# A new head for an attention and two-layer kernel: finer first chunks from two queues, norms and softmax beside the scores, two blocks interleaved

## The chip, the core and the metric

The kernel runs on one core of one Trainium2 chip. Its time is the device time of one execution in microseconds (us); the number given for a kernel is the median of several executions. A profiled execution stands beside it: the hardware profiler records every instruction of the engines (TensorE, called PE in the rows, its weight loads PEld; VectorE, DVE; ScalarE, ACT; GpSimd, POOL; and the queue of SyncE, SPq) and every packet of the DMA engines.

## The reference

Everything is in float32. Attention is over the channels, not the tokens: with N = 6016 tokens and C = 256 channels, the scores are a 256x256 matrix, summed over all tokens. Two gated layers follow, token by token.

```python
def _attn_ref(q, k, v, tau):            # q, k, v: 1 x 6016 x 256
    qn = q / (np.linalg.norm(q, axis=1, keepdims=True) + 1e-06)
    kn = k / (np.linalg.norm(k, axis=1, keepdims=True) + 1e-06)
    s = kn.transpose(0, 2, 1) @ qn / tau
    s = s - s.max(-1, keepdims=True)
    a = np.exp(s)
    a /= a.sum(-1, keepdims=True) + 1e-09
    return (v @ a).astype(np.float32)

def _moe_ref(x, w_gate, w_val, w_out, rms_g):    # 256 -> 1536 -> 256
    rms = np.sqrt(np.mean(x * x, axis=-1, keepdims=True) + 1e-06)
    xn = x / rms * rms_g
    g = xn @ w_gate
    silu = g * (1.0 / (1.0 + np.exp(-g)))
    val = xn @ w_val
    return (silu * val @ w_out).astype(np.float32)

def _moe2_ref(x, w_in, w_out):                   # 256 -> 2048 -> 256
    h = x @ w_in
    g = h - np.tanh(h)
    return (g @ w_out).astype(np.float32)
```

## The kernel before

**Scores (L276 to L349).** q and k lie with 47 tokens on each of the 128 partitions. A tile is one token per partition, 128 x 256 of q and of k. A chunk is 1, 2 or 4 tiles, loaded by one DMA for q and one for k, all from SP's queue, with four buffers each. For each tile TensorE multiplies k's two halves of 128 channels with q (L308); each float32 product runs as two passes on the engine, so a tile is four passes. Beside it ACT squares the chunk (L325) and DVE adds the squares into `acc` (L326), which has room for 4 tiles; at the end `acc` is folded to 2 tiles (L328), and products with a column of ones (L345) give the squared norms of the channels in `nrm`. The products for the last two chunks stand behind the norm products. DVE turns the norms into reciprocals with an integer seed and three Newton steps (`rsqrt_ops`, L93 to L96) on 128x8 numbers.

**Softmax (L363 to L392).** The reciprocal norms of q have to lie along the free dimension. DVE scales an identity by them (`dq`), a product with ones spreads them to all partitions (L370), ACT copies them to SBUF. Then for the two halves of the rows in turn: scale, row maximum, exponential with row sum, reciprocal of the sum, scale. The result is `a_full`.

**The weights.** They come as 64-bit floats seen as pairs of 32-bit integers, in chunks of 512 columns. The generator `conversion` (L172) makes float32 of them and splits each into a high and a low half, in steps: ACT `w_start` (L136), DVE shift (L183), DVE `w_low` of the chunk before (L78), DVE and/or (L189), DVE shift/or (L195), ACT high half (L75). `pump(n)` issues n steps; the table `PLAN` says how many stand at which label (`at("s", i)` after score chunk i, `at("c", k)` in the middle part, `at("g", ...)`, `at("h", ...)` in the layers). `need(...)` issues steps until the weights it names exist: the gate asks for the column block two ahead. The order of the chunks is wg0, wv0, w10, wg1, wv1, w11, wg2, ... `W_LOADS` says after which score chunks the first five are loaded.

**The middle part (L654 to L692) and the layers.** The tokens are cut into 12 blocks of 512. For blocks 0 and 1 x = v a is a full float32 product (L412); ACT squares it, narrow products (L479) give the mean squares per token, DVE the reciprocal root, and again an identity scaled on DVE (`diag`, L491) and a product with ones (L497) spread it. The normalised x is split into a high and a low half (`x0h`, `x0l`; block 1 `x1h`, `x1l`), and each product of the layers is three products of halves (`mm3`, L82 to L84). The gate runs column by column, block 0 three columns ahead of block 1; the steps of block 1's x (`post`) are issued between the columns of block 0, so many after each as `POST` says. Every engine executes its instructions in the order in which they are written. At most 8 DMAs are under way at once; the one that takes a completion counter waits for the one that had it.

What the prediction speaks of is in these functions:

Of the kernel before, what the change touches and what calls it, by code (L numbers as in the profile page):

```python
# [16 lines left out]
P = 128  # L17
# [15 lines left out]
def attn_moe_kernel(  # L33
# [132 lines left out]
    LAST_CHUNKS, FOLD = [4, 2, 1], 1  # L166
    BEHIND = 2
    W_LOADS = [1, 3, 5, 9, 11]
# [107 lines left out]
    def attention():  # L276
        with ExitStack() as st:
# [3 lines left out]
            for n in [1, 2, 1] + [W] * ((NT - W - 1) // W - 1) + LAST_CHUNKS:  # L281
                chunks.append((t, n))
                t += n
            assert t == NT
            H = W // 2
# [3 lines left out]
            S = [psum(f"S{m}") for m in range(KC)]  # L289
            raw = {}  # L290
            NCH = len(chunks)
# [11 lines left out]
            def scores(i):  # L303
                n = chunks[i][1]
                qt, kt = raw.pop(i)
                for j in range(n):
                    for m in range(KC):
                        nc.tensor.matmul(  # L308
                            S[m][:, :C], kt[:, j, m * P:(m + 1) * P], qt[:, j, :],
                            start=(i == 0 and j == 0), stop=(i == NCH - 1 and j == n - 1))  # L310
# [6 lines left out]
            nrm = psum("nrm")  # L317
            for i, (t0, n) in enumerate(chunks):
                for s in range(2):
# [6 lines left out]
                    nc.vector.tensor_add(out=acc[:, s, :n], in0=acc[:, s, :n], in1=sq[:, :n])  # L326
                if t0 + n == NT - sum(LAST_CHUNKS[FOLD:]):
# [467 lines left out]
```

## Time and profile before

| | |
|---|---|
| runs | 1206.48, 1207.55, 1207.74 us; median 1207.55 |
| profiled execution | 1206.14 us, its span 1204.30 us |
| PE busy | 1186.8 us (99% of the span) |
| DVE busy | 681.1 us (57%) |
| ACT busy | 536.2 us (45%) |
| DMA, first 10 us / 20 to 30 us | 215 / 416 GB/s |

The span is what the engines' records cover; 1.84 us of the execution lie around it. The busy shares are means over 1204 us; the change is in the first 100 us, where DVE is busy for 7 to 9 of every 10 us and the DMA engines are full from 12 to 40 us.

### The profile page before, as it was taken

How to read it: one execution, taken by the hardware profiler on the slowest of the kernel's cores; microseconds unless marked ns; L12 is line 12 of the kernel's file. 1: busy time of each engine (PE TensorE's matmuls, PEld its weight loads, DVE VectorE, ACT ScalarE, POOL GpSimd, SP SyncE). 2: the span in 40 equal slices, each digit the busy share in tenths (PEclk: the TensorE clock that was granted, in tenths of full speed). 3: DMA queues.
4: the chain of work that ended last, by engine and by line, in shares of the span. 5: the costliest groups of instructions: out<-in, count | busy, mean ns of one | idle time of the engine just before them, and what ended most of it. 6: DMA issues, size and time to landing. Idle time of an engine off the chain costs nothing.

```text
span 1204.3 us, 13571 instructions
## 1 busy us (share of the span) xinstructions
PE 1186.8 (99%) x5310; PEld 988.9 (82%) x5310; DVE 681.1 (57%) x1119; ACT 536.2 (45%) x930; POOL 0.7 (0%) x6
## 2 busy tenths in 40 slices
PE   8889999999999999999999999999999999999998
PEld 6668888888888888888888888888888888888998
DVE  5888779653384384375356347347337437436534
ACT  6556556543343354254344344344335325425434
POOL 0000000000000000000000000000000000000000
PEclk9999999999999999999999999999999999999999
DMA  9534332001001000000000000100100000000000
GB/s 340 208 107 123 89 104 88 18 19 35 1 1 36 1 1 20 16 1 18 18 1 18 18 1 1 35 1 1 35 1 1 32 1 1 18 1 1 18 1 14
DMA packets 20640, 43.33 MB, mean 36 GB/s; under 512 B 1889, under 2 KB 3169, under 8 KB 20577
## 3 DMA queue, kind: packets, MB, share of 16 engines
q1 hardware_dynamic: 20576, 42.48, 10.5%
q8 instruction: 41, 0.67, 0.2%
q14 instruction: 23, 0.18, 0.0%
HBM read 36.31 MB, written 6.16 MB: 35 GB/s over the span
## 4 chain that ended last, share of the span: by engine, by line
PE 97%; DVE 1%; DMA 1%; ACT 0%; issue 0%; SPq 0%; DVEq 0%
PE h L84 7%; PE h L82 7%; PE out L82 7%; PE out L84 7%; PE out L83 7%; PE h L83 7%; PE g L82 5%; PE y L84 5%; PE y L82 5%; PE g L84 5%; PE y L83 5%; PE g L83 5%; PE v L82 5%; PE v L84 5%; PE v L83 5%; PE S L308 3%
## 5 line engine op out<-in xcount | busy, mean ns | idle before, releaser
L546 DVE TENSOR_TENSOR t<-t,v 128x512 f32<-128x512 f32 (+1 forms) x144 | 97.4, 676 | 227.9 <-PE v L84 219.4
L560 DVE TENSOR_TENSOR t<-h,t 128x512 f32<-128x512 f32 (+1 forms) x192 | 129.6, 675 | 48.9 <-ACT t L559 48.8
L545 ACT ACTIVATE t<-g 128x512 f32<-128x512 f32 (+1 forms) x144 | 84.6, 588 | 129.5 <-PE g L84 126.5
L559 ACT ACTIVATE t<-h 128x512 f32<-128x512 f32 (+1 forms) x192 | 110.5, 575 | 17.3 <-PE h L84 17.1
L308 PE MATMUL S<-q,k 128*128 128x256 f32 x188 | 43.9, 394 | 5.5 <-DMA k<-k_in 5.5
L308 PEld LDWEIGHTS S<-q,k 128*128 128x128 f32 x188 | 36.7, 198 | 11.9 <-DMA q<-q_in 4.3
L326 DVE TENSOR_TENSOR acc<-acc,sq 128x1024 f32<-128x1024 f32 (+2 forms) x24 | 26.4, 1113 | 14.7 <-ACT sq L325 14.3
L96 DVE SCALAR_TENSOR_TENSOR y<-sq,y 128x512 f32<-128x512 f32 (+1 forms) x27 | 18.0, 668 | 0.0
L93 DVE SCALAR_TENSOR_TENSOR sq<-y,sq 128x512 f32<-128x512 f32 (+1 forms) x27 | 18.0, 668 | 0.0
L95 DVE TENSOR_TENSOR sq<-sq,y 128x512 f32<-128x512 f32 (+1 forms) x27 | 18.0, 667 | 0.0
L325 ACT ACTIVATE sq<-q 128x1024 f32<-128x1024 f32 (+2 forms) x12 | 11.6, 967 | 11.3 <-DMA q<-q_in 9.3
L443 ACT ACTIVATE xg<-x,g_t 128x512 f32<-128x512 f32 (+1 forms) x24 | 15.9, 667 | 1.1 <-PE ms L479 1.1
L75 ACT ACTIVATE u_2h<-t 128x512 fp32r<-128x512 f32 (+1 forms) x12 | 7.5, 623 | 18.5 <-DVE t L546 18.5
L75 ACT ACTIVATE w_12h<-t 128x512 fp32r<-128x512 f32 (+1 forms) x12 | 7.5, 623 | 18.5 <-DVE t L560 14.4
L75 ACT ACTIVATE u_8h<-t 128x512 fp32r<-128x512 f32 (+1 forms) x12 | 7.5, 623 | 18.2 <-DVE t L546 18.2
L75 ACT ACTIVATE u_1h<-t 128x512 fp32r<-128x512 f32 (+1 forms) x12 | 7.5, 623 | 18.1 <-DVE t L546 18.1
L75 ACT ACTIVATE u_6h<-t 128x512 fp32r<-128x512 f32 (+1 forms) x12 | 7.5, 623 | 18.1 <-DVE t L546 18.1
L75 ACT ACTIVATE u_9h<-t 128x512 fp32r<-128x512 f32 (+1 forms) x12 | 7.5, 624 | 17.7 <-DVE t L546 17.7
L75 ACT ACTIVATE u_7h<-t 128x512 fp32r<-128x512 f32 (+1 forms) x12 | 7.5, 623 | 17.7 <-DVE t L546 17.7
L75 ACT ACTIVATE u_10h<-t 128x512 fp32r<-128x512 f32 (+1 forms) x12 | 7.5, 623 | 17.7 <-DVE t L546 17.7
L75 ACT ACTIVATE u_0h<-t 128x512 fp32r<-128x512 f32 (+1 forms) x12 | 7.5, 623 | 17.3 <-DVE t L546 17.3
L75 ACT ACTIVATE u_5h<-t 128x512 fp32r<-128x512 f32 (+1 forms) x12 | 7.5, 624 | 17.2 <-DVE t L546 17.2
(2051 smaller groups left out, 3602.7 us busy)
## 6 DMA issues: line engine op xcount, KB each, us to landing
vraw<-vT_in SPq DMA_DIRECT2D x11, 512.0 KB, 3.8
outT<-o SPq DMA_DIRECT2D x22, 256.0 KB, 2.0
q<-q_in SPq DMA_DIRECT2D x10, 512.0 KB, 7.1
k<-k_in SPq DMA_DIRECT2D x10, 512.0 KB, 7.9
q<-q_in SPq DMA_DIRECT2D x2, 256.0 KB, 3.6
k<-k_in SPq DMA_DIRECT2D x2, 256.0 KB, 3.9
wg0raw<-w_gate_in SPq DMA_DIRECT2D x1, 512.0 KB, 8.9
wv0raw<-w_val_in SPq DMA_DIRECT2D x1, 512.0 KB, 9.6
```

What stands on the lines that cost most here:

```text
L75: nc.scalar.activation(out=dst, in_=src, func=AF.Copy, scale=scale)
L82: nc.tensor.matmul(out, wh, xh, start=first, stop=False)
L83: nc.tensor.matmul(out, wl, xh, start=False, stop=False)
L84: nc.tensor.matmul(out, wh, xl, start=False, stop=last)
L93: lambda: nc.vector.scalar_tensor_tensor(out=t, in0=y, scalar=-0.5, in1=m, op0=ALU.mult, op1=ALU.mult),
L95: lambda: nc.vector.tensor_mul(out=t, in0=t, in1=y),
L308: nc.tensor.matmul(S[m][:, :C], kt[:, j, m * P:(m + 1) * P], qt[:, j, :], start=(i == 0 and j == 0), stop=(i == NCH - 1 and j == n - 1))
L326: nc.vector.tensor_add(out=acc[:, s, :n], in0=acc[:, s, :n], in1=sq[:, :n])
L545: nc.scalar.activation(out=t[:, :n], in_=g[:, :n], func=AF.Silu)
L546: nc.vector.tensor_mul(out=t[:, :n], in0=t[:, :n], in1=v[:, :n])
L559: nc.scalar.activation(out=t[:, :n], in_=o[:, :n], func=AF.Tanh)
L560: nc.vector.tensor_sub(out=t[:, :n], in0=o[:, :n], in1=t[:, :n])
```

## The change

The diff, cut to what is spoken of; of the table two lines.

```diff
 PLAN = {
-    ('s', 7): 1, ('s', 8): 1, ('s', 9): 1, ('s', 10): 1, ('s', 11): 1, ('c', 0): 2, ('c', 1): 3,
...
+    ('s', 8): 1, ('s', 9): 2, ('s', 10): 2, ('s', 11): 2, ('s', 12): 1, ('c', 0): 1, ('c', 1): 1,
...
-    LAST_CHUNKS, FOLD = [4, 2, 1], 1
-    BEHIND = 2
-    W_LOADS = [1, 3, 5, 9, 11]
+    FIRST_CHUNKS, LAST_CHUNKS = [1, 1, 2, 2, 2], [2, 1]
+
+    BEHIND = 3
+    WARM = 5
...
-                    r = sp.tile([P, W, C], F32, tag=f"raw{nm}", bufs=4, name=f"{nm}{i}")
-                    nc.sync.dma_start(out=r[:, :n, :], in_=src[:, t0:t0 + n, :])
+                    if i < NF:
+                        tag, bufs = small[2 * i + s]
+                        r = act.tile([P, W // 2, C], F32, tag=tag, bufs=bufs, name=f"{nm}{i}")
...
+                    (nc.scalar if s and i < NF else nc.sync).dma_start(
+                        out=r[:, :n, :], in_=src[:, t0:t0 + n, :])
...
-            for i in range(4):
+            for i in range(NF + 2):
                 load(i)
             nc.sync.dma_start(out=tau_t, in_=tau.to_broadcast([P, 1]))
             nc.sync.dma_start(out=g_t, in_=rms_g)
+            w_load(w_queue[0], sp, EARLY_RAW)
+            load(NF + 2)
+            load(NF + 3)
+            w_load(w_queue[1], sp, EARLY_RAW)
+            load(NF + 4)
+            for _ in range(WARM):
+                nc.tensor.matmul(nrm[:, :P], ones, ones, start=True, stop=True)
...
-                    nc.vector.tensor_add(out=acc[:, s, :n], in0=acc[:, s, :n], in1=sq[:, :n])
-                if t0 + n == NT - sum(LAST_CHUNKS[FOLD:]):
-                    nc.vector.tensor_add(out=acc[:, :, :H], in0=acc[:, :, :H], in1=acc[:, :, H:])
+                    if i < NCH - BEHIND:
+                        add(acc[:, s, :n], acc[:, s, :n], sq[:, :n])
+                        continue
+                    for h in (2, 1):
+                        if n >= 2 * h:
+                            add(sq[:, :h], sq[:, :h], sq[:, h:2 * h])
+                    add(acc[:, s, 0], acc[:, s, 0], sq[:, 0])
+                if i == NCH - BEHIND - 1:
+                    for h in (2, 1):
+                        add(acc[:, :, :h], acc[:, :, :h], acc[:, :, h:2 * h])
...
-                load(i + 4)
-                if i in W_LOADS:
...
-                if i == NCH - 4:
+                if i >= NF:
+                    load(i + 5)
+                if i + 5 == NCH - 1:
                     load_v(0)
+                    w_load(w_queue[2])
+                    w_load(w_queue[3])
                     load_v(1, "ah")
+                    w_load(w_queue[4])
                 at("s", i)
...
+            rest = [(i, j) for i in range(NCH - BEHIND, NCH) for j in range(chunks[i][1])]
+            for i, j in rest:
+                score(i, j, 0)
             at("c", 0)
...
+            for x, (i, j) in enumerate(rest):
+                if x == 1:
+                    for m in range(KC):
+                        nc.tensor.matmul(
+                            rq_ps[:, m * P:(m + 1) * P], r_[:, 2 * m:2 * m + 1].to_broadcast([P, P]),
+                            ident, start=True, stop=True)
+                score(i, j, 1)
...
+                nc.vector.tensor_tensor_reduce(
+                    out=s_, in0=S[m][:, :C], in1=rq, scale=1.0, scalar=-3.4028234e38, op0=ALU.mult,
+                    op1=ALU.max, accum_out=mx)
...
+                nc.vector.tensor_scalar_mul(out=a_full[m], in0=e_, scalar1=sm)
+
+            nc.scalar.activation(out=mx, in_=ones[:, :1], func=AF.Silu)
...
-        def diag():
...
         def spread():
             T["y"] = psum(f"r{b}")
-            nc.tensor.matmul(T["y"][:, :n], ones, T["d"][:, :n], start=True, stop=True)
+            for t in range(NG):
+                nc.tensor.matmul(
+                    T["y"][:, t * P:(t + 1) * P], T["yn"][:, 2 * t:2 * t + 1].to_broadcast([P, P]),
+                    ident, start=True, stop=True)
...
+        x_full((0, 0, 0), (0, 1, 0), (1, 0, 0), (0, 0, 1), (0, 1, 1))
         for c in range(KC):
-            xs[0].append(x_matmuls_full(0, c))
             p0["square"](c)()
+            p0["ms"](c)
+        at("c", 3)
+        x_full((1, 1, 0), (1, 0, 1), (1, 1, 1))
...
-        POST = [8, 4, 9]
+        POST = [6, 5, 9]
```

The chunks are now 1, 1, 2, 2, 2, nine times 4, 2, 1 tiles. The first five k chunks are started from ACT's queue, and the first ten chunks of q and k have buffers of their own, ahead of any release. The last three chunks (4, 2 and 1 tiles) stand behind the norm products: first the seven products of each with the first half of k's channels, then those with the second half. `acc` is folded to one tile and the last chunks' squares are folded before they are added. The spreads take the reciprocals as a broadcast stationary operand against the identity. The x products of blocks 0 and 1 are issued by halves of a, those of the first half of a ahead.

What stands where, at three places. First ACT, at the end of the score chunks: q_229/k_231 and q_250/k_252 are the last whole chunks before, followed by 2 tiles and 1 tile, and `w10y` is the conversion of chunk w10, whose raw bits are `w10raw`. Before:

```order
L325 ACTIVATE sq_0_321<-q_250 128x1024
L325 ACTIVATE sq_1_324<-k_252 128x1024
L325 ACTIVATE sq_0_336<-q_271 128x512
L325 ACTIVATE sq_1_339<-k_273 128x512
L325 ACTIVATE sq_0_342<-q_294 128x256
L325 ACTIVATE sq_1_345<-k_296 128x256
L136 ACTIVATE w10y<-w10raw 128x512
L75 ACTIVATE wv0h<-wv0y 128x512
```

After, from chunk 11 on (q_210 is chunk 11, q_228 chunk 12, q_246 chunk 13, q_267 chunk 14):

```order
L344 ACTIVATE sq_0_308<-q_210 128x1024
L344 ACTIVATE sq_1_311<-k_212 128x1024
L137 ACTIVATE w10y<-w10raw 128x512
L344 ACTIVATE sq_0_328<-q_228 128x1024
L344 ACTIVATE sq_1_331<-k_230 128x1024
L76 ACTIVATE wv0h<-wv0y 128x512
L344 ACTIVATE sq_0_346<-q_246 128x1024
L344 ACTIVATE sq_1_351<-k_248 128x1024
L344 ACTIVATE sq_0_356<-q_267 128x512
```

w10's conversion stood behind the last square and stands now ahead of those of chunks 12 to 15.

Second SP's queue, where w10raw is loaded. Before, among the chunks:

```order
L300 DMA q_191<-q_in 128x1024
L300 DMA k_193<-k_in 128x1024
L130 DMA w10raw<-w_out_in 128x2x512
L300 DMA q_211<-q_in 128x1024
L300 DMA k_213<-k_in 128x1024
```

After, at the end of them (q_291 is the last chunk, vraw_295 block 0 of v):

```order
L312 DMA q_291<-q_in 128x256
L312 DMA k_293<-k_in 128x256
L261 DMA vraw_295<-vT_in 128x2x512
L131 DMA w10raw<-w_out_in 128x2x512
L131 DMA wg1raw<-w_gate_in 128x2x512
L261 DMA vraw_301<-vT_in 128x2x512
```

The load of w10 has moved behind all of q and k and behind v's first block.

Third DVE at the start of the gate, from block 0's second low half (`x0l`) to the low half of the first gate column's result (`u_0l`). Before:

```order
L78 TENSOR_TENSOR x0l<-xg_0_475,x0h 128x512
L78 TENSOR_TENSOR al_558<-a_418,ah_557 128x256
L78 TENSOR_TENSOR al_562<-a_422,ah_561 128x256
L546 TENSOR_TENSOR t_0_581<-t_0_581,v_0_568 128x512
L78 TENSOR_TENSOR wg2l<-wg2y,wg2h 128x512
L189 SCALAR_TENSOR_TENSOR wv2y<-wv2raw,wv2y 128x512
L78 TENSOR_TENSOR u_0l<-t_0_581,u_0h 128x512
```

After:

```order
L79 TENSOR_TENSOR x0l<-xg_0_481,x0h 128x512
L79 TENSOR_TENSOR wg1l<-wg1y,wg1h 128x512
L79 TENSOR_TENSOR al_539<-a_425,ah_538 128x256
L79 TENSOR_TENSOR al_543<-a_436,ah_542 128x256
L191 SCALAR_TENSOR_TENSOR wv1y<-wv1raw,wv1y 128x512
L197 SCALAR_TENSOR_TENSOR wv1y<-wv1raw,wv1y 128x512
L185 TENSOR_SCALAR w11y<-w11y 128x512
L79 TENSOR_TENSOR wv1l<-wv1y,wv1h 128x512
L574 TENSOR_TENSOR t_0_573<-t_0_573,v_0_549 128x512
L191 SCALAR_TENSOR_TENSOR w11y<-w11raw,w11y 128x512
L197 SCALAR_TENSOR_TENSOR w11y<-w11raw,w11y 128x512
L79 TENSOR_TENSOR u_0l<-t_0_573,u_0h 128x512
```

Two conversion steps stood here (of wg2 and wv2), and seven stand here now (of wg1, wv1 and w11).

## Rows read from the trace of the kernel before

**Rows 1.** TensorE's waits, whole span: us in total, times, longest.
```profile
PE S L308 <- DMA k<-k_in: 5.5, 4, 3.4
PE x L412 <- ACT a L392: 3.9, 1, 3.9
```

**Rows 2.** Timeline, end of the scores: start, us, engine, line, op, tiles, forms.
```profile
15.24 31.32 PE L308 MATMUL S<-q,k 128*128 128x256 f32 x144 [0.59 <-DMA k<-k_in]
...
45.62 0.42 DVE L326 TENSOR_TENSOR acc<-acc,sq 128x256 f32<-128x256 f32 x1
...
46.39 1.84 PE L345 MATMUL nrm<-ones,acc 128*128 128x2 f32 x16
```

**Rows 3.** Timeline, gate and block 1's operands.
```profile
77.97 0.69 DVE L546 TENSOR_TENSOR t<-t,v 128x512 f32<-128x512 f32 x1 [2.24 <-PE v L84]
...
86.14 1.13 PE L497 MATMUL r<-d,ones 128*128 128x512 f32 x2 [1.48 <-DVE d L491]
...
87.34 0.39 PE L83 MATMUL g<-x0h,wg1l 128*128 128x512 f32 x1
...
88.00 0.68 DVE L505 TENSOR_TENSOR xg<-xg,r 128x512 f32<-128x512 f32 x1
...
91.36 0.69 DVE L78 TENSOR_TENSOR x1l<-xg,x1h 128x512 fp32r<-128x512 f32 x1 [0.70 <-ACT x1h L75]
...
92.34 0.39 PE L84 MATMUL g<-x1l,wg0h 128*128 128x512 f32 x1
```

**Rows 4.** Stretches, busy us of each engine, clock, DMA share, GB/s; DMA to 42 us.
```profile
0.00:12.00 12.00, 7.13 (x21) 5.24 (x22) 1.81 (x5) 6.21 (x9) 0.70 (x6) 1.00 0.73 224
12.00:24.00 12.00, 11.41 (x54) 9.74 (x53) 8.70 (x8) 7.44 (x8) 0.00 (x0) 1.00 1.03 416
...
DMA packets 5681, 14.44 MB, mean 344 GB/s; under 512 B 828, under 2 KB 1568, under 8 KB 5680
```

**Rows 5.** Groups by form, 0 to 90 us: busy us, mean ns of one.
```profile
L326 DVE TENSOR_TENSOR acc<-acc,sq 128x1024 f32<-128x1024 f32 x20 | 24.3, 1224 | 14.5 <-ACT sq L325 14.3
L325 ACT ACTIVATE sq<-k 128x1024 f32<-128x1024 f32 x10 | 10.6, 1057 | 1.7 <-DMA k<-k_in 1.7
...
L443 ACT ACTIVATE xg<-x,g_t 128x512 f32<-128x512 f32 x4 | 2.6, 689 | 1.1 <-PE ms L479 1.1
...
L75 ACT ACTIVATE x0h<-xg 128x512 fp32r<-128x512 f32 x2 | 1.3, 632 | 1.0 <-DVE xg L505 1.0
...
L136 ACT ACTIVATE w10y<-w10raw 128x512 f32<-128x512 f32 x1 | 0.7, 660 | 0.0
```

**Rows 6.** Timeline, softmax to block 0's operands.
```profile
51.16 0.20 DVE L362 RECIPROCAL r__385<-y__369 128x8 f32<-128x8 f32 x1
...
52.74 0.38 ACT L373 ACTIVATE rq<-rq_ps 128x256 f32<-128x256 f32 x1 [4.15 <-PE rq_ps L370]
...
56.64 8.45 PE L412 MATMUL x<-vraw,a 128*128 128x512 f32 x12 [3.94 <-ACT a L392]
...
73.46 0.80 PE L82 MATMUL g<-x0h,wg0h 128*128 128x512 f32 x1 [1.44 <-ACT x0h L75]
...
73.59 1.48 DVE L78 TENSOR_TENSOR x0l<-xg,x0h 128x512 fp32r<-128x512 f32 x2
```

**Rows 7.** Stretches after the softmax and at the gate; the clock is the column after POOL.
```profile
56.00:58.00 2.00, 1.36 (x2) 0.84 (x3) 1.38 (x5) 1.90 (x6) 0.00 (x0) 0.50 0.00 0
...
62.00:64.00 2.00, 2.00 (x5) 0.84 (x4) 1.66 (x4) 1.87 (x4) 0.00 (x0) 0.81 0.69 216
...
76.00:78.00 2.00, 2.00 (x9) 1.60 (x9) 0.03 (x1) 0.85 (x2) 0.00 (x0) 0.89 0.02 6
```

**Rows 8.** Timeline, DVE between the gate and block 1.
```profile
82.47 0.68 DVE L195 SCALAR_TENSOR_TENSOR wv2y<-wv2raw,wv2y 128x512 int32<-128x512 int32 x1
...
83.07 0.42 DVE L183 TENSOR_SCALAR w12y<-w12y 128x512 int32<-128x512 int32 x1
...
85.21 0.87 DVE L491 TENSOR_SCALAR d<-ident,nary 128x128 f32<-128x128 f32 x4
```

More of the change, by code (lines that the diff above doesn't have):

```diff
@@ L280, in attention @@
             W = 4
-            for n in [1, 2, 1] + [W] * ((NT - W - 1) // W - 1) + LAST_CHUNKS:
+            whole = (NT - sum(FIRST_CHUNKS) - sum(LAST_CHUNKS)) // W
+            for n in FIRST_CHUNKS + [W] * whole + LAST_CHUNKS:
                 chunks.append((t, n))
                 t += n
-            assert t == NT
-            H = W // 2
+            assert t == NT and sum(FIRST_CHUNKS[:3]) == W
+            NCH, NF = len(chunks), len(FIRST_CHUNKS)
+            LENT = [NF + 4, NF + 9]
+            small = [("xs", 6)] * 6 + [("ul", 3)] * 3 + [("u", 5)]
             qr = q.rearrange("(p n) c -> p n c", p=P)
@@ L289, in attention @@
             S = [psum(f"S{m}") for m in range(KC)]
+            nrm = psum("nrm")
             raw = {}
-            NCH = len(chunks)
             def load(i):
@@ L388, in attention @@
-            for m in range(KC):
-                nc.vector.tensor_scalar_add(out=sm[m], in0=sm[m], scalar1=1e-9)
-                nc.vector.reciprocal(out=sm[m], in_=sm[m])
+                rk = r_[:, 2 * (KC + m):2 * (KC + m) + 1]
+                s_ = sp.tile([P, C], F32, tag="s", bufs=2, name=f"s{m}")
+                mx = sp.tile([P, 1], F32, tag="mx", bufs=2, name=f"mx{m}")
+                e_ = sp.tile([P, C], F32, tag="e", bufs=2, name=f"e{m}")
+                sm = sp.tile([P, 1], F32, tag="sm", bufs=2, name=f"sm{m}")
@@ L405, in attn_moe_kernel, with x_matmul_full @@
     xn = {}
-    def x_matmuls_full(b, c):
+    def x_matmul_full(o, b, c, kk):
         n = blocks[b][1]
-        o = psum(f"x{b}_{c}")
-        for kk in range(KC):
-            nc.tensor.matmul(
-                o[:, :n], a_full[kk][:, c * P:(c + 1) * P], v_raw[b][:, kk, :n], start=kk == 0,
-                stop=kk == KC - 1)
-        return o
+        nc.tensor.matmul(
+            o[:, :n], a_full[kk][:, c * P:(c + 1) * P], v_raw[b][:, kk, :n], start=kk == 0,
+            stop=kk == KC - 1)
     def x_matmuls(b, c):
@@ L473, in x_post, with ms_narrow @@
         NG = n // P
-        def ms_narrow():
-            o = T["o"] = psum(f"ms{b}")
-            for t in range(NG):
-                for c in range(KC):
+        def ms_narrow(*cs):
+            for c in cs or range(KC):
+                if c == 0:
+                    T["o"] = psum(f"ms{b}")
+                for t in range(NG):
                     nc.tensor.matmul(
-                        o[:, 2 * t:2 * t + 2], T[f"sq{c}"][:, t * P:(t + 1) * P], mean32,
-                        start=c == 0, stop=c == KC - 1)
+                        T["o"][:, 2 * t:2 * t + 2], T[f"sq{c}"][:, t * P:(t + 1) * P], mean32,
+                        start=c == 0 and t == 0, stop=c == KC - 1 and t == NG - 1,
+                        skip_group_check=True)
         def eps_narrow():
@@ L517, in x_post @@
                 square=square, gain=gain, ms=ms_narrow,
-                rs=[eps_narrow] + [rs(i) for i in range(10)] + [diag], spread=spread, norm=norm,
-                high=high, low=low)
+                rs=[eps_narrow] + [rs(i) for i in range(10)], spread=spread, norm=norm, high=high,
+                low=low)
         return ([square(c) for c in cs] + [sq_sum] + [gain(c) for c in cs]
@@ L682, in attn_moe_kernel @@
             p0["high"](c)()
-            at("c", 5 + c)
+            p1["gain"](c)()
+        for c in range(KC):
+            p1["ms"](c)
         for c in range(KC):
             p0["low"](c)()
+        at("c", 7)
         split_a()
```

96 lines of the change are left out of this document (37 added, 59 removed), and 7 rows, old and new, of the table PLAN.

## The prediction

> **What bounds the kernel now.** I read the time by engine first, then TensorE's waits, then the first 100 us by stretches and instruction by instruction. TensorE is busy for nearly the whole span, and after 87.34 its products follow one another to the end: every wait that the list has lies before 100 us [rows 1]. So a change to the head is worth what it moves the point from which TensorE no longer waits, and the rest of the span moves with it. Up to that point before loses time at four places: the first chunks (5.5 us of waits for data), the softmax (3.9), TensorE's lower clock after it and again at the gate, and DVE's work before block 1.
>
> The second thing to see is DVE. In the head it is close to a bound of its own. Its last norm addition ends at 46.04 and TensorE starts the norm products at 46.39, straight from the scores [rows 2]: scores and norm additions end together. From 78 to 92 us DVE goes without a pause from one instruction to the next; block 1's second low half ends at 92.05 and the product that reads it starts at 92.34 [rows 3], a slack of about 0.25 us. A head in which TensorE has less to wait for gains only if DVE arrives earlier as well.
>
> **The early chunks, the second queue and the warm-up products.** They lie beside other work. The norm products stand behind chunk 12's scores on TensorE. If nothing at all were won early, 8 of the 47 tiles would be done at 15.24 as now, and the 32 tiles to the end of chunk 12, four passes each at 31.32/144 = 0.217 us [rows 2], would end at 15.24 + 27.8 = 43.1. What DVE needs, below, is about 51.5. So I count 0 for these edits on TensorE; the cover is 8 us, and if it were gone they would be worth at most 4.9 us: 32 passes of 0.217 from 3.40 end at 10.3 instead of 15.24. They do bear on when data arrive.
>
> **The wait for w10raw, the first term.** In the new order ACT converts w10 ahead of chunk 12's squares, and w10's load now stands on SP behind every q and k chunk and the first v block. ACT is in order: chunk 12's, 13's, 14's and 15's squares stand behind that instruction, DVE's additions behind the squares, and the norm products behind the additions. Before, w10 was loaded in the middle of the chunks and converted after all squares.
>
> When does it land (call it L)? Ahead of it and with it go 12.32 MB of q and k, 1.05 MB of w_gate and w_val, 0.52 of v and 0.52 of itself: 14.42 MB. Before moves 14.44 MB in 42 us, the last of them held back by TensorE; 224 GB/s, 2.69 MB, in the first 12 us, 416 GB/s from 12 to 24 [rows 4]. Lowest: 416 from 2.0 us on, L = 36.7. By the rates of the rows: 12 us as now and 416 after, 40.2. Highest: before's own course, 42. I take 39.5, near the middle one, since the early rate is the only one that rows show, and a little under it for the issues of two engines. "DMA: Bandwidth & Descriptors" of the Trainium skill (Issuing engines are not separate DMA queues) says that starting DMAs from several engines saves only the time to start them, because all run on the same 16 DMA engines; by that rule L is 40.2 and the time 0.7 us later. The trace of before has one queue only and can't say.
>
> From L, with the durations of [rows 5] and 60 to 100 ns from engine to engine: w10's conversion 0.66, chunk 12's squares 1.06 each, so DVE starts at L+1.9 and has before it: two additions of 1.22 (the second waits for its square), the two folds 1.22 and 0.69 (DVE takes 0.69 for 512 elements, 0.42 for 256 [rows 2, 3]), one conversion step 0.42, chunk 13 twice 0.69+0.42+0.42, chunk 14 twice 0.42+0.42, chunk 15 twice 0.42. With the overlap of about 0.08 us that independent neighbours show this is 10.2 us: the last addition ends at L+12.05 = 51.55. The q half of the norms has started by then; TensorE, idle since 43 or earlier, is at the lower clock, so the last norm product ends near L+13.2 = 52.7, against 48.23 before [rows 2]. **+4.5 us.** Of it the wait itself is 5.05: chunk 11's k lands 9.4 us before w10, DVE is through with that chunk and its two conversion steps at L-3.2, and idle to L+1.86.
>
> **From the norms to block 0's operands, the second term.** Before takes from 48.23 to the start of the second low half of x0 at 74.38 (two within 1.48 from 73.59 [rows 6]): 26.15 us. After, counted from the norms' end: 14 passes of the last scores, first half, at first at the lower clock, 0.43 us each. The granted clock is 0.81 in 62 to 64 and 0.89 in 76 to 78, so the step from 1.2 to 2.4 GHz is near 62.8 and 76.4: 6.1 us after the restart at 56.64 and 3.0 after that at 73.46 [rows 6, 7]. I take 5 after the restart at 51.2, so 3.5 us of low clock (8 passes) and 6 passes of 0.217: 4.8. The reciprocal norms (3.1 in before, 48.23 to 51.36) are hidden beneath. Two passes of the second half and the spreading of q's norms 0.9. From the copy of the spread norms to the first usable attention row block before takes 3.9 (52.74 to 56.64), with both blocks' products and maxima ahead of it; with one block's, 2.9 (not shown in the trace: the fused product and maximum; between 0.48, its product alone, and 0.90, product and separate maximum; I take 0.65). The other 12 passes of scores (2.6 us) run beneath. Five x products of two passes, 0.43 each: 4.3. A square, no longer than the gain's 0.69 [rows 5], and block 0's second mean products, 8 passes of 0.115 [rows 2], with their waits: 1.75. Three more x products 2.6, the spread of 8 short passes 0.9. Then norm 0.68, high half 0.63, block 1's gain 0.69, high half 0.63 and waits: 2.75. Sum 20.8 instead of 26.15. **-5.4 us.** Bounds: 1.0 less or 0.6 more for the clock, which costs half a microsecond for each one, 0.25 for the fused instruction.
>
> **The conversions left over, the third term.** The new order runs 17 conversion steps ahead of the gate instead of 28. The 11 others, and one more, don't vanish: the gate asks for the chunk two columns ahead, so they run on DVE between x0's second low half and block 1's first norm. Counted in the order: 18 steps there instead of 6, of the 12 more nine of 0.60 to 0.72 and three of 0.34 (start to start a little below the durations, as from 82.47 to 83.07): 6.65. Block 1's diagonal, 0.87, is gone [rows 8]: +5.8. Before has a pause of 2.24 there, for the first v product [rows 3], which is filled, but new short pauses come, where a low half waits for its high half on ACT: together I count 0.65 back. So from x0's second low half to block 1's second low half it is 16.98 (74.38 to 91.36) + 5.8 - 0.65 = 22.1. **+5.15.** Bounds 4.0 (no new pause) and 6.0 (no pause filled).
>
> The slack of 0.25 comes off. Sum: +4.5 - 5.4 + 5.15 - 0.25 = **+4.0 us** at the first place from which TensorE runs densely. What follows has the same order on both engines. From the profiled execution, 1206.14 (span 1204.30 and 1.84 around it), this makes 1210.1; that run stands 1.41 below the median of the runs, 1207.55, so I forecast **1211.5**, slower. Its own range by the bounds (L 2.8 less or 2.5 more, the two other terms about 1 each, not all at once) is 1208 to 1215.
>
> **Rivals.** *The clock falls again before block 1.* By the walk TensorE waits some 2.9 us, 82.8 to 85.7, for the spread of block 1. The idle stretch of 3.94 us before 56.64 let it fall to 1.2 GHz, that of 1.48 before 86.14 did not [rows 3, 6, 7]. If it falls and rises only 6.1 us later, the spread and the next 18 products at 0.43 still end before x1 is there, but block 1's first 12 products take 12 x 0.2 = 2.4 us more: 1213.9.
>
> *w10raw is in time.* For it: DMA is no longer short of chunks early, and 8 transfers are under way at once. Against: even 416 GB/s from the first byte gives 36.7, and ACT comes to that instruction near L-7, after chunk 11's squares. Without the wait 5.05 go: +4.0 - 5.05, 1206.5, no change that can be told.
>
> *The gate hides the conversions (faster).* If DVE reaches block 1's operands before TensorE wants them, TensorE is dense from the gate on. It starts at 72.4 by the walk, then 42 products of 0.227, the spread and one product more: 10.7 us, 83.1, where before is at 87.34 [rows 3]: -4.25, 1203.3. It decides from the point where DVE comes to block 1's first norm by 84 instead of 92. For it: 2.24 us of pause. Against: 5.8 us more work on an engine that is already without a pause.
>
> **Chances.** Forecast 0.52, clock 0.18, no wait 0.17, gate dense 0.13. A measurement of this kernel tells 0.2%, 2.4 us, from no change. Of the forecast's share five sixths lie above 1210.0, with the clock rival and a little of the third this is 0.63 slower; 0.09 of the forecast and 0.11 of the no-wait case make 0.20 the same; 0.17 faster. The range 1205 to 1216 leaves out most of the dense gate and the far end of the clock rival.
>
> **What would show it.** Right: ACT idle for microseconds ahead of L137 on w10y, released by DMA; L373 starting near 51; TensorE without a wait in the x products; DVE without a pause from 75 to 95 with block 1's norm (L533) near 92; a wait of TensorE ahead of L523 and ahead of block 1's first gate product. Wrong: w10y released by an instruction on ACT or DVE; L373 before 48; block 1's first gate product before 91.2. The walk fails by the clock if the granted clock in 52 to 60 is at its upper level throughout.

## The result, and the profile after

The changed kernel is slower: 1215.48 us median (1212.43 to 1216.25, 5 runs) against 1207.55 of before beside it, ratio 1.006 with a 95% interval of 1.0043 to 1.0077. The forecast was 1211.5 us, slower, in a range of 1205 to 1216. The profiled execution took 1215.48 us; its span is 1212.8 us, 8.5 more than before's 1204.3 (2.7 us lie around it, 1.8 in before). One experiment's profile (e10, the second with the early part undone) was taken at a granted clock of 0.85 and its times inside the span aren't used; all comparisons leave out such executions, and two of 5770 and 6872 us.

TensorE's waits in the whole span of the changed kernel (us in total, times, longest), against [rows 1]:

```profile
PE nrm L373 <- DVE acc L323: 11.4, 1, 11.4
PE g L83 <- ACT x1h L76: 3.4, 2, 2.7
PE S L318 <- DMA k<-k_in: 1.8, 2, 1.5
PE nrm L335 <- DVE ones L228: 1.1, 1, 1.1
PE r L523 <- DVE nary L97: 0.9, 1, 0.9
```

The waits for data (5.5 us) and for the softmax (3.9) have shrunk or gone. In their place stand 11.4 us ahead of the norm products and 3.4 us for block 1's operands: the first ends on DVE's work, the second on ACT behind DVE. The timeline around the end of the scores (start, us, engine, line, op, tiles, in brackets the idle time before and what ended it), against [rows 2]:

```profile
8.59 33.32 PE L318 MATMUL S<-q,k 128*128 128x256 f32 x152 [1.52 <-DMA k<-k_in]
...
35.07 0.33 SPq L312 DMA_DIRECT2D q<-q_in  x1
...
36.40 0.46 SPq L131 DMA_DIRECT2D w10raw<-w_out_in  x1
...
41.66 0.66 ACT L137 ACTIVATE w10y<-w10raw 128x512 f32<-128x512 f32 x1 [7.41 <-DMA w10raw<-w_out_in]
...
43.30 2.36 DVE L323 TENSOR_TENSOR acc<-acc,sq 128x1024 f32<-128x1024 f32 x2 [5.61 <-ACT sq L344]
...
53.34 1.87 PE L373 MATMUL nrm<-ones,acc 128*128 128x2 f32 x8 [11.43 <-DVE acc L323]
```

TensorE is through with the scores that stand ahead of the norms at 41.9, 4.7 us sooner than before; 3.5 of that come from 16 more passes that now stand behind the norm products. ACT then sits 7.4 us before w10's conversion, and DVE 5.6 us before chunk 12's additions. The norm products end at 55.21, against 48.23: 7 us lost in one place. From there to block 1 (same columns), against [rows 3, 6, 8]:

```profile
62.20 0.38 ACT L402 ACTIVATE rq<-rq_ps 128x256 f32<-128x256 f32 x1 [8.75 <-PE rq_ps L397]
62.62 0.42 DVE L411 CUSTOM_DVE_ANT_0 s<-S,rq 128x256 f32<-128x256 f32 x1 [4.29 <-ACT rq L402]
...
64.86 4.56 PE L443 MATMUL x<-vraw,a 128*128 128x512 f32 x10
...
77.28 0.69 DVE L79 TENSOR_TENSOR x0l<-xg,x0h 128x512 fp32r<-128x512 f32 x1 [0.40 <-ACT x0h L76]
...
89.25 1.16 PE L523 MATMUL r<-ident,nary 128*128 128x128 f32 x8 [0.95 <-DVE nary L97]
...
95.81 0.68 DVE L533 TENSOR_TENSOR xg<-xg,r 128x512 f32<-128x512 f32 x1
97.20 0.50 PE L83 MATMUL g<-x1h,wg0h 128*128 128x512 f32 x1 [2.68 <-ACT x1h L76]
...
99.17 0.69 DVE L79 TENSOR_TENSOR x1l<-xg,x1h 128x512 fp32r<-128x512 f32 x1 [0.70 <-ACT x1h L76]
...
100.21 0.63 PE L85 MATMUL g<-x1l,wg0h 128*128 128x512 f32 x1
...
102.66 0.39 PE L83 MATMUL y<-u_2h,w11h 128*128 128x512 f32 x1
```

The x products start without a wait, as meant. From the norms' end to x0's second low half it is 22.07 us instead of 26.15; from there to x1's second low half 21.89 instead of 16.98. The last row's product, the first that reads w11, is the last place that I lay side by side: it starts at 93.93 before and at 102.66 after, 8.73 later, which is the span's difference but for 0.2. The stretches (busy us of PE, PEld, DVE, ACT, POOL; then granted clock, DMA share, GB/s), against [rows 4, 7]:

```profile
0.00:12.00 12.00, 9.18 (x34) 7.64 (x35) 2.50 (x7) 6.17 (x11) 0.70 (x6) 1.00 0.81 281
12.00:24.00 12.00, 11.97 (x56) 10.25 (x55) 8.60 (x9) 7.96 (x8) 0.00 (x0) 1.00 0.95 374
52.00:60.00 8.00, 6.66 (x20) 5.67 (x21) 4.82 (x20) 0.76 (x3) 0.00 (x0) 0.50 0.01 2
60.00:62.00 2.00, 2.00 (x10) 1.74 (x9) 0.00 (x0) 0.00 (x0) 0.00 (x0) 0.73 0.00 0
78.00:80.00 2.00, 2.00 (x6) 1.59 (x6) 1.97 (x5) 1.01 (x3) 0.00 (x0) 0.53 0.00 0
100.00:102.00 2.00, 2.00 (x6) 1.60 (x6) 2.00 (x5) 1.51 (x3) 0.00 (x0) 0.50 0.00 0
```

After the wait of 11.4 us TensorE has the lower clock (1.2 GHz) until about 61 us, then once more in block 0's first gate products (0.53 from 78 to 80 us), and again behind the wait for x1h.

### The profile page after: what moved, and what is told of

It is laid out like the page before. It is cut to its first block, busy times and chain, and to the rows that moved or that the text cites. A ratio compares the mean times of both kernels' runs of the same rounds, so it can differ in the third digit from the quotient of the medians.

```text
span 1212.8 us, 13610 instructions
## 1 busy us (share of the span) xinstructions
PE 1190.8 (98%) x5332; PEld 994.0 (82%) x5332; DVE 679.9 (56%) x1116; ACT 535.2 (44%) x931; POOL 0.7 (0%) x6
## 4 chain that ended last, share of the span: by engine, by line
PE 95%; DVE 2%; DMA 1%; ACT 1%; issue 0%; SPq 0%; ACTq 0%; DVEq 0%
PE h L85 7%; PE h L83 7%; PE out L83 7%; PE out L85 7%; PE out L84 7%; PE h L84 7%; PE y L85 5%; PE y L84 5%; PE y L83 5%; PE g L83 5%; PE v L85 5%; PE v L84 5%; PE v L83 5%; PE g L85 5%; PE g L84 5%; PE S L318 3%
## 5 line engine op out<-in xcount | busy, mean ns | idle before, releaser
L76 ACT ACTIVATE u_3h<-t 128x512 fp32r<-128x512 f32 (+1 forms) x12 | 7.5, 623 | 17.3 <-DVE t L574 17.3
L76 ACT ACTIVATE w_9h<-t 128x512 fp32r<-128x512 f32 (+1 forms) x12 | 7.5, 623 | 17.1 <-DVE t L588 15.5
```

The source lines that it names most:

```text
L76: nc.scalar.activation(out=dst, in_=src, func=AF.Copy, scale=scale)
```

## The experiments

Theory: the wait for w10raw and the conversion steps left over make the changed kernel slow. Rivals: the norms are late for another reason (DVE's small additions, data); the steps are hidden under the gate; the finer chunks or the second queue cost time themselves; the clock alone does it. All runs are in one table. Each ratio is to before's runs on the same chip; the last four columns are starts in the profiled execution (x0l and x1l are the low halves of block 0's and block 1's x).

| run | median us | ratio to before, 95% | norm products start | x0l, second | x1l, second | w11's first product |
|---|---|---|---|---|---|---|
| before | 1207.55 | | 46.39 | 74.38 | 91.36 | 93.93 |
| after | 1215.48 | 1.0043 to 1.0077 | 53.34 | 77.28 | 99.17 | 102.66 |
| e1_w10_early | 1211.14 | 1.0021 to 1.0044 | 50.84 | 74.51 | 96.39 | 100.42 |
| e6_w10_behind | 1206.19 | 0.9970 to 0.9990 | 45.66 | 67.69 | 89.60 | 93.63 |
| e4_one_queue | 1216.05 | 1.0049 to 1.0076 | 53.68 | 77.52 | 99.42 | 103.44 |
| e9_early_undone | 1212.98 | 1.0023 to 1.0049 | 50.00 | 72.55 | 94.45 | 96.92 |
| e10_early_undone2 | 1214.60 | 1.0047 to 1.0075 | | | | |
| e2_conv_left_out | 1209.43 | 1.0006 to 1.0023 | 53.42 | 76.11 | 93.95 | 96.44 |
| e5_steps_in_gap | 1212.94 | 1.0024 to 1.0050 | 54.02 | 77.75 | 98.09 | 101.99 |
| e7_both_moved | 1206.11 | 0.9974 to 0.9992 | 45.30 | 71.83 | 90.69 | 93.15 |
| e8_clock_kept | 1211.34 | 1.0013 to 1.0036 | 54.62 | 74.95 | 96.86 | 100.76 |
| e11_gate_clock | 1205.03 | 0.9970 to 0.9987 | 45.60 | 68.25 | 90.15 | 92.64 |
| e12_low_on_gpsimd | 1208.23 | 0.9995 to 1.0013 | 46.22 | 70.81 | 93.12 | 95.60 |
| e13_two_fills | 1202.79 | 0.9941 to 0.9968 | 44.81 | 65.61 | 87.52 | 89.99 |

**The wait for w10.** First only its load is moved:

```diff
+                if i + 5 == NCH - 3:
+                    w_load(w_queue[2])
                 if i + 5 == NCH - 1:
                     load_v(0)
-                    w_load(w_queue[2])
```

> The changed kernel with one edit: w10's load is put on the SP queue behind chunk 13's loads instead of behind the last chunk's; nothing else moves. Theory (the wait of ScalarE for w10raw, 7.4 us in the changed kernel, is what makes the norm products late): w10 lands before about 38 us, ScalarE's wait is under 1 us, the norm products start at 48 to 50 us instead of 53.3, and the time falls by 4 to 5 us, to 1210.5 to 1211.5. Rival (the norms are late anyway, because VectorE has nine small additions and a conversion step more to do behind the last chunks, or because w10's 0.5 MB now delay the last q and k): the norm products start no earlier than 52 us and the time stays within 1.5 us of the changed kernel's 1215.5.

A third of the delay is gone, not nearly all of it. ACT still waits, and the norm products start 2.5 us earlier, not 3.3 to 5.3. The time fell by 2.1 us between the profiled executions, which both had a mean granted clock of 0.990; the 4.3 us between medians came out as expected, but the two kernels' executions differ in clock (below). Rows of the timeline and of SP's DMA issues:

```profile
29.30 0.42 SPq L131 DMA_DIRECT2D w10raw<-w_out_in  x1
...
39.44 0.68 ACT L137 ACTIVATE w10y<-w10raw 128x512 f32<-128x512 f32 x1 [4.93 <-DMA w10raw<-w_out_in]
...
50.84 1.87 PE L374 MATMUL nrm<-ones,acc 128*128 128x2 f32 x8 [8.65 <-DVE acc L323]
```

Issued 7.1 us earlier, w10 lands 2.2 us earlier: it now needs 10.1 us, where the late one needed 5.2. The chunks issued just ahead of it, at 28.44 and 28.86, need 8.5 and 9.3 us too, with the DMA engines at a share of 1.02 to 1.04 from 28 to 36 us. So moving the load isn't a cure. Next the instruction that waits is moved:

```diff
-    ('s', 8): 1, ('s', 9): 2, ('s', 10): 2, ('s', 11): 2, ('s', 12): 1, ('c', 0): 1, ('c', 1): 1,
+    ('s', 8): 1, ('s', 9): 2, ('s', 10): 2, ('s', 11): 0, ('s', 12): 0, ('c', 0): 1, ('c', 1): 1,
...
             nc.vector.reciprocal(out=r_, in_=y_)
+            pump(3)
```

> The changed kernel with the three conversion steps behind chunks 11 and 12 moved behind the reciprocal of the norms (the step that starts w10's conversion now stands behind the last square on ScalarE); w10's load stays where it is, and as many steps stand before the gate. The run with the earlier load had shortened ScalarE's wait only from 7.4 to 4.9 us and the norms by 2.5. Theory (the wait is the whole cause of the late norms): ScalarE no longer waits for w10raw ahead of the squares, VectorE goes through its additions as chunks 12 to 15 land, the norm products start at 45.5 to 47 us instead of 53.3, and the time falls by 6 to 7.5 us, to 1208 to 1209.5, so within 2 us of the kernel before. Rival (behind the wait, the additions of the last chunks bound the norms, as in before): the products start at 50 to 52, and the time is 1212 or more.

The theory holds, and the gain is larger than expected: 9.3 us instead of 6 to 7.5, to 0.1 to 0.3% below before. ACT's conversion stands behind the last square with no wait, and TensorE's wait is 3.8 us instead of 11.4:

```profile
45.66 1.23 PE L373 MATMUL nrm<-ones,acc 128*128 128x2 f32 x8 [3.79 <-DVE acc L323]
...
45.67 0.65 ACT L137 ACTIVATE w10y<-w10raw 128x512 f32<-128x512 f32 x1
```

The norm products start 7.7 us earlier: the 5.6 us for which DVE had waited, and some 1.8 of conversion steps (0.69, 0.69, 0.42) that no longer stand ahead of its last additions. So the edit moved two things at once, the wait and the steps. In this run DVE's additions go from 33.90 to 46.22 without more than 0.2 us of pause; now they are the bound.

**The early part.** One queue instead of two:

```diff
-                    (nc.scalar if s and i < NF else nc.sync).dma_start(
+                    nc.sync.dma_start(
```

> The changed kernel with the first five chunks of k issued from SP like q, and none from ScalarE. Theory (the second queue is worth nothing at the end: VectorE's additions, behind the wait for w10, set the norms): the first 12 us move fewer bytes and the scores start up to 1 us later, but the norm products start within 0.5 us of 53.3 and the time is within 1 us of 1215.5. Rival A (the second queue hurts, by taking ScalarE's time or by mixing two streams): 1213.5 or less. Rival B (the landing of w10 hangs on what moved in the first 12 us, since SP's later loads wait for scores): about 2 us later, 1217 or more.

The time is 0.6 us longer, which can't be told from none. w10's conversion starts at 42.30 instead of 41.66, the norm products at 53.68 instead of 53.34; but three other runs with both queues have that conversion at 41.72 (e2), 42.33 (e5) and 42.90 (e8). The first 12 us move 262 GB/s, against 277 to 295 in the ten profiles with two queues.

The whole early part undone, one queue as above and:

```diff
-    FIRST_CHUNKS, LAST_CHUNKS = [1, 1, 2, 2, 2], [2, 1]
+    FIRST_CHUNKS, LAST_CHUNKS = [1, 2, 1], [2, 1]
...
-    WARM = 5
+    WARM = 0
```

> The changed kernel with its early part undone: first chunks of 1, 2, 1 groups as before instead of 1, 1, 2, 2, 2, all loads from SP, no warm-up products. Theory (the early part is worth nothing at the end, since the norms wait for w10 and VectorE): scores start 1 to 3 us later, w10's landing and the norm products move by under 1 us, and the time is within 1 us of 1215.5. Rival (the early part brings the last chunks and w10 in earlier): 2 us or more slower, 1217.5 or more.

It is 2.5 us faster, against the theory (the profiled execution, 1209.0, is the lowest of the five). The edit wasn't clean: this kernel has 15 chunks, and the table of conversion steps goes by chunk number, so one full chunk less stands behind w10's conversion. From it to the norm products it is 7.1 us here, 11.7 in the changed kernel. With the table moved by one:

```diff
-    ('s', 8): 1, ('s', 9): 2, ('s', 10): 2, ('s', 11): 2, ('s', 12): 1,
+    ('s', 7): 1, ('s', 8): 2, ('s', 9): 2, ('s', 10): 2, ('s', 11): 1,
```

> The run with the early part undone again (first chunks 1, 2, 1, one queue, no warm-up), now with the conversion steps counted from the end: that kernel has 15 chunks of q and k, not 16, and the table names steps by chunk, so that in the first such run w10's conversion stood ahead of the last three chunks, not the last four (norm products at 50.0 us, time 1213.0). Here it stands ahead of the last four again. Theory (the early part is worth nothing at the end; the 2.5 us of that run came from the shifted step): norm products at 53 to 55 us, time 1215 to 1217. Rival (the finer chunks, the second queue or the warm-up cost time themselves): norm products at 50 to 51, time 1213 or less.

It is 1214.60 us, 0.9 below the changed kernel, within the spread of either, and between what theory (1215 to 1217) and rival (1213 or less) expected: the early part neither helps nor hurts by an amount that can be told here. At a like mean clock (0.993) it took 1213.3 to 1214.7 us and the changed kernel 1212.4 and 1213.1, so 1 us for the early part isn't ruled out. Where the norm products start in this kernel isn't shown.

**The steps left over.** The shift, and the two combines in the same way, are left out for three weight chunks (wv1, w11, wg2), which are then not rebuilt:

```diff
+    LEAVE = (4, 5, 6)
...
-            nc.vector.tensor_single_scalar(
+            if i not in LEAVE:
+              nc.vector.tensor_single_scalar(
                     out=y, in_=y, scalar=3, op=ALU.logical_shift_left)
```

> The changed kernel without the three integer steps on VectorE (shift, two combines; 0.42 + 0.69 + 0.69 us) for the chunks wv1, w11 and wg2: these weights are then not rebuilt, so this run leaves out part of the computation. All else stays. Theory (the conversion steps left over fill VectorE between block 0's second low half and block 1's norm, and set when block 1's first product starts): 5.4 us of VectorE work go, nearly all of it between 73 and 95 us; the stretch from the end of x0's last low half to x1's last low half falls from 21.9 to 17 to 18 us and the time by 4 to 5 us, to about 1211. Rival (TensorE's products of block 0's first two steps set that stretch): the stretch stays at 21 to 22 us, and the time within 1 us.

It is 6.05 us less, where 4 to 5 were expected. From x0's to x1's second low half it takes 17.84 us instead of 21.89: 4.05 for 5.4 us of instructions, the remainder going into waits for other engines. The other 2 us are the clock's: in this profile it was back at its upper level near 58.5 instead of 61, and it didn't fall behind block 1's wait. The first of these can't come from the edit, which touches nothing ahead of 70 us. Now five more conversion steps are put behind the reciprocal of the norms:

```diff
             nc.vector.reciprocal(out=r_, in_=y_)
+            pump(5)
```

> The changed kernel with five more conversion steps placed behind the reciprocal of the norms, where VectorE idles 4.3 us until rq is copied (58.3 to 62.6 us). Theory (each conversion step not done before the gate costs its 0.6 us behind it): five of the twelve leftover steps are gone from the stretch between block 0's low half and block 1's norm, which falls from 21.9 to about 19; rq is still copied at about 62.2; the time falls by 2.5 to 3.5 us, to 1212 to 1213. Rival 1 (VectorE does not bound that stretch): within 1 us of 1215.5. Rival 2 (the steps' halves on ScalarE stand ahead of the copy of rq and delay the softmax): rq later by over 1 us, and no gain or a loss.

It is 2.5 us less, as expected, but the stretch shrank only by 1.55, to 20.34, where about 2.9 were expected: DVE waits there 2.0 us for the gate's first v product, at the lower clock.

```profile
81.95 0.69 DVE L575 TENSOR_TENSOR t<-t,v 128x512 f32<-128x512 f32 x1 [2.00 <-PE v L85]
```

Both edits together (pump(8) in the w10 run):

> The run before this one (w10's conversion behind the squares) with five more conversion steps behind the reciprocal, eight in all, so that five fewer are left for the gate. Theory (the two costs, the wait and the leftover steps, add up): the gains of the two single edits add, 6 to 7.5 us and 2.5 us, and the time is 1205.5 to 1207, no slower than the kernel before. Rival (they share a cover: once the norms are early, rq is early too and eight steps do not fit ahead of it): rq's copy waits for VectorE's or ScalarE's steps and the time stays at 1208 or above.

It is 1206.11 us, within the theory's 1205.5 to 1207, but the w10 edit alone had 1206.19, so the five further steps bring nothing: the gains don't add, and the rival's mechanism holds, though not its time (1208 or more). Eight steps don't fit. The spread that rq is copied from ends at 53.16, but the copy stands on ACT behind conversion steps and starts at 54.73 (52.61 with three steps), and DVE's first softmax product comes behind a conversion step of its own at 55.47 (53.03 with three). TensorE waits, and its clock falls (0.50 from 58 to 60 us):

```profile
54.73 0.36 ACT L403 ACTIVATE rq<-rq_ps 128x256 f32<-128x256 f32 x1
...
55.47 0.42 DVE L412 CUSTOM_DVE_ANT_0 s<-S,rq 128x256 f32<-128x256 f32 x1
...
57.71 4.54 PE L444 MATMUL x<-vraw,a 128*128 128x512 f32 x6 [1.96 <-DVE a L424]
```

The stretch before block 1 is 3.0 us shorter (18.86), but block 0's operands come 4.1 later.

**The clock.** 52 products of ones by ones in TensorE's wait:

```diff
+            for _ in range(52):
+                nc.tensor.matmul(nrm[:, :P], ones, ones, start=True, stop=True)
             NN = 2 * 2 * KC
```

> The changed kernel with 52 products of ones by ones (128x128, written over by the norm products) on TensorE between the scores it has done by 41.9 us and the norm products at 53.3 us, so that TensorE doesn't idle in the wait; they take about 0.21 us each at the full clock. Theory (the low clock between 44 and 61 us, after TensorE's idle time, costs the stretch behind the norms): the granted clock stays at 1.00 through 62 us, the rest of the scores runs at the full clock, rq is copied about 58.5 instead of 62.2 us, and the time falls by 3 to 4 us, to about 1212. Rival 1 (the chain of VectorE's small steps sets that stretch, not TensorE): rq no more than 1 us earlier, time within 1 us of 1215.5. Rival 2 (the products only move the low clock to the gate): rq earlier, but the gate slower, and no gain at the end.

It is 4.1 us less, with the norm products even 1.3 us later. The stretches of this run and the copy of rq:

```profile
44.00:52.00 8.00, 8.00 (x74) 8.00 (x73) 7.25 (x11) 4.62 (x6) 0.00 (x0) 1.00 0.24 92
...
56.00:62.00 6.00, 6.00 (x31) 5.32 (x30) 3.96 (x21) 1.38 (x4) 0.00 (x0) 1.00 0.00 0
...
59.87 0.38 ACT L405 ACTIVATE rq<-rq_ps 128x256 f32<-128x256 f32 x1 [5.16 <-PE rq_ps L400]
```

From the norm products' start to rq it is 5.25 us instead of 8.86, and from rq on to x0's second low half 15.08 in both. The second rival (the low clock only moves to the gate) shows in part: it falls at block 1's spread (0.50 from 88 to 90 us), but the stretch is 21.91 all the same. Such products at block 1's first product too, on top of the w10 edit:

```diff
+        if (b, f) == (1, 0):
+            for _ in range(12):
+                nc.tensor.matmul(g[:, :P], ones, ones, start=True, stop=True)
```

> The run with w10's conversion behind the squares, and 12 products of ones by ones on TensorE ahead of block 1's first gate product, where it waits 2.7 us for x1h; after that wait the granted clock was 0.53 between 88 and 92 us and 0.62 between 92 and 96. Theory (the clock that falls behind this wait costs time; of the prediction's rivals the one on the clock): it stays at 1.00 through 96 us, the 18 products behind it take 0.23 us each instead of 0.43, and the time falls by 1.5 to 2.5 us, to 1204 to 1205. Rival (the wait comes from VectorE, which is then waited for again a little later): the products run faster but wait for their next operand, and the time stays within 0.7 us of 1206.2.

It is 1.2 us less between medians (expected 1.5 to 2.5); by the ratios to before, 0.9980 and 0.9979, the gain can't be told from none. Inside the profile the mechanism shows: from x1's second low half to w11's first product it is 2.49 us instead of 4.03. But in four other runs (e2, e7, e9, e12) the clock doesn't fall there and the stretch is 2.46 to 2.49 without any fill. First the run without the products, then this one:

```profile
88.00:92.00 4.00, 3.53 (x9) 2.14 (x8) 3.30 (x7) 2.19 (x4) 0.00 (x0) 0.53 0.00 0
```
```profile
88.00:92.00 4.00, 4.00 (x27) 3.29 (x26) 3.14 (x6) 1.77 (x4) 0.00 (x0) 1.00 0.00 0
```

**Low halves on GpSimd**, on top of the w10 edit:

```diff
-        lo_of(c["l"], c["y"], c["h"])
+        sub = nc.gpsimd.tensor_sub if 3 <= w_queue.index(c) < 8 else nc.vector.tensor_sub
+        sub(out=c["l"], in0=c["y"], in1=c["h"].bitcast(F32))
```

> The run with w10's conversion behind the squares, and the low halves of five weight chunks (wg1, wv1, w11, wg2, wv2; a subtraction of 128x512, 0.69 us each on VectorE) on GpSimd. VectorE has no pause between block 0's second low half (68.4 us) and block 1's norm (86.2). Theory (VectorE's queue sets when block 1's norm comes): 5 times about 0.62 us go from it, the stretch falls by about 3 us, and the time by 2 to 3 us, to 1203.5 to 1204.5. Rival (GpSimd takes several us for each, or slows VectorE while it works; no trace here shows it at such work): the gate's products wait for low halves, the stretch is as long or longer, and the time 1206 or more.

It is 2.0 us more: no gain, as the rival said. From x0's to x1's second low half it is 22.3 us instead of 21.9: the 3.1 us taken from DVE came back as slower instructions and waits. Another 0.9 us are lost ahead of it (rq to x0's second low half, 15.98 instead of 15.08). The remainder isn't shown to come from the edit: rq comes 8.6 us behind the norm products' start instead of 7.0, because the clock was low until after 53 us. GpSimd's subtraction takes 1.29 us, and a small DVE instruction that meets it ends with it, at 79.15 (0.17 us elsewhere):

```profile
77.84 1.29 POOL L142 TENSOR_TENSOR w11l<-w11y,w11h 128x512 fp32r<-128x512 f32 x1 [2.02 <-ACT w11h L76]
78.01 1.14 DVE L94 SCALAR_TENSOR_TENSOR nart<-nary,narm 128x8 f32<-128x8 f32 x1
```

At 65.08 a Newton step of 0.17 takes 1.20, and at 84.93 a combine of 0.69 takes 1.65, in the same way. "SBUF — State Buffer" of the Trainium skill (SBUF: two separate sides) says that a VectorE operation with two inputs in SBUF and a GpSimd operation share a pair of ports, which the first to start holds to its end. The rows shown agree: the subtraction starts first, and both end within 0.02 us.

**A version that beats both.** The w10 edit, the 12 products ahead of block 1, and 18 ahead of the norm products:

> The last version but one (w10's conversion behind the squares, 12 products of ones ahead of block 1's first gate product; 1205.0 us) with 18 more such products ahead of the norm products, where TensorE waits 3.9 us for VectorE's last addition and the granted clock then falls to 0.50. Theory (the low clock behind the norms costs there as it did in the changed kernel, where filling the wait brought rq 4 us nearer to the norm products' start than... that is 5.3 instead of 8.9 us behind it): the clock stays at 1.00 through the rest of the scores, rq is copied 6 us behind the norm products' start instead of 7.6, and the time falls by 1 to 1.5 us, to 1203.5 to 1204. Rival (VectorE's conversion steps ahead of the softmax now bound it, since rq comes before they are done): rq's copy or the first product of the softmax waits for them, and the time stays within 0.5 us of 1205.

It is 1202.79 us, 0.32 to 0.59% below before, and 2.2 below the version with 12 products (expected 1 to 1.5). rq comes 5.4 us behind the norm products' start, and the clock stays at 1.00 from 44 to 76 us. The rival shows at one place: rq's copy ends at 50.58, and DVE takes it up at 50.95, straight from a conversion step:

```profile
50.22 0.36 ACT L406 ACTIVATE rq<-rq_ps 128x256 f32<-128x256 f32 x1
...
50.95 0.42 DVE L415 CUSTOM_DVE_ANT_0 s<-S,rq 128x256 f32<-128x256 f32 x1
```

## Why the prediction was right, and what was mis-sized

**What bounds the kernel.** The prediction said that a change to the head is worth what it moves the point from which TensorE is dense. Profiled time less the start of w11's first product is 1111.9 to 1113.7 us in the 13 profiles that are used (before 1206.14 - 93.93 = 1112.2, after 1112.8). Right. The signs that the prediction named came too: ACT idle ahead of w10's conversion until the DMA's end, the x products without a wait, and waits ahead of L523 (0.95) and of block 1's first product (2.68); only later than it named them (L373 at 53.34 instead of 51, L533 at 95.81 instead of 92).

| term | forecast | profile after |
|---|---|---|
| wait for w10raw, norms' end | +4.5 | +6.98 (48.23 to 55.21) |
| norms' end to x0's second low half | -5.4 | -4.08 (26.15 to 22.07) |
| to x1's second low half | +5.15 | +4.91 (16.98 to 21.89) |
| to its product | -0.25 | +0.06 (92.34 to 100.21 in all) |
| low clock behind it (a rival) | 0 | +0.86 |
| sum | +4.0 | +8.73 |

**Early chunks, second queue, warm-up: 0.** Right, as far as can be told: the scores ahead of the norms end at 41.9 (43.1 by the walk, had nothing been won), and TensorE waits that much longer. Undone, the time changes by 0.9 us.

**First term: right mechanism, too small by 2.5.** From L to the norms' end the walk gave 13.2 us, the trace 13.6. L itself, when w10 lands, was 41.6, not 39.5. The step "when does it land" summed bytes by rates and took the transfers to be always under way. But SP puts w10 behind the last chunk, and that chunk's buffer comes free when TensorE has done chunk 10's scores: SP issues the last three q chunks at 28.16, 31.61 and 35.07, 3.45 us apart, which is TensorE's 16 passes of 0.217. w10 was issued at 36.40 and took 5.2 us; in five other runs it was issued between 36.46 and 37.86 and took 5.0 to 5.3. The bytes alone don't explain 41.6: the DMA engines had moved 12.8 MB by 36 us, and at 416 GB/s the 14.42 would have been there at 39.8, but from 36 to 38 us they moved only 287 GB/s. The 39.4 of the first experiment don't confirm the sum either, since there 1.3 MB less (chunks 14 and 15 and v's block) were issued ahead of w10. By the rule of "DMA: Bandwidth & Descriptors" of the Trainium skill (Issuing engines are not separate DMA queues) the prediction's estimate of L was 40.2. L was 42.3 with one queue and 41.7 to 42.9 in four runs with two, later than by either estimate, and no gain of the second queue shows at this point. The rival without the wait was put at 1206.5, and the run without it took 1206.2; that these agree is luck, since the rival took 5.05 us off a forecast of 1211.5 and the run took 9.3 off 1215.5, 1.8 of it by other steps.

**Second term: right walk, wrong clock.** The walk of 20.8 us had 8 score passes at the lower clock, 8 x (0.43 - 0.217) = 1.7; without them 19.1. With the clock kept up the run takes 74.95 - 55.83 = 19.1, and none of the walk's steps is off by more than 0.3 us. In the changed kernel the clock rose near 61, 7.7 us after the restart, not 5, and the stretch cost 2.95 more than at the full clock. (The recorded terms add up to 20.9, not 20.8, which is rounding.) The fused product and maximum was put at 0.65 and takes 0.47 with its read-out (62.62 to the next instruction at 63.09).

**Third term: right, by 0.24.** The 21.9 us are DVE's: they come out between 21.88 and 21.91 in eight runs whatever TensorE's clock and the start of the stretch (after, e1, e4, e6, e8, e9, e11, e13), with and without the low clock at 78 to 81 us, and at 17.84, 18.86 and 20.34 where steps are taken out.

**The slack of 0.25** did not come off (+0.06): block 1's second low half ends at 99.86 and its product starts at 100.21, behind two products at the lower clock.

**The rivals.** The clock fell before block 1, as that rival said, but behind the wait for x1h instead of that for the spread, and for 0.9 us, not 2.4 (up to 1.5 in other runs). In e9, e11, e12 and e13 TensorE did wait 2.6 to 3.0 us for the spread; the clock fell there and was back ahead of block 1's products, which cost nothing. In e6 the same wait was not followed by a fall until 88 us. A dense gate didn't come: DVE reached block 1's first norm at 95.8, not by 84.

So two errors of size, 2.5 and 1.3 us, one rival's 0.9 and the slack's 0.3 point the same way, with 0.2 against them: 8.7 instead of 4.0 inside the profile. Between medians it is 7.9, twice the forecast's 4.0.

**What was luck.** The mechanism was right, but the time is only 0.5 us inside the stated range and 0.5 outside the 1208 to 1215 that the bounds gave. How near the edge it came hung on the clock of single executions, which the prediction took as one fixed number: three of the changed kernel's five had a mean granted clock of 0.990 and took 1215.5 to 1216.3 us, the other two 0.993 and 1212.4 and 1213.1. Before, measured beside e6, splits as well: 1206.6 to 1208.2 at 0.994, 1209.1 to 1209.7 at 0.991 to 0.993. So some 3 us between two medians can be the clock's, and gains of one or two microseconds rest on the profiles more than on the medians.

## What to carry to other kernels

An instruction for later work that waits for a late load must not stand ahead of urgent work on an in-order engine; move the instruction, since moving the load won back only a third of the delay. When a load is queued behind others whose buffers free late, count its issue, not its bytes. A wait of TensorE costs twice, in the wait and in the clock behind it: cheap products in the wait gave 4.1 us back at the norms in the changed kernel, and two such fills together 3.4 on top of the w10 edit (e6 to e13).

## What the runs showed of the hardware that was not expected

The time from TensorE's restart to the full clock isn't one number: 3.0 and 6.1 us in before, 7.7 in the changed kernel, 5.1 in the run with steps left out, which restarts at 53.42 with the same instructions, and 4.9 and 7.4 in e9 and e12. A 128x512 subtraction on GpSimd, 1.27 to 1.46 us, held up DVE instructions with two inputs by up to 1.03 us. The second DMA queue raised the first 12 us from 262 GB/s to 277 to 295, and no gain of it was left when w10 landed.
